# Another order, engine split and PSUM placement for a written-out schedule: two long convolutions and two MLPs on one core

## The chip, the cores and the metric

The kernel runs on one core of a Trainium2 chip. The core has five engines with a queue each: PE (TensorE, matrix products out of SBUF into PSUM), ACT (ScalarE), DVE (VectorE), POOL (GpSimd) and SP, which here only issues DMAs. PSUM has eight banks of 2 KB on each of 128 partitions. The metric is the time of one execution on the device in microseconds (us), lower is better. Three runs of the kernel before took 241.83, 242.24 and 243.01 us: the median is 242.24.

## What is computed

The reference, cut to the computation (S = 2048 tokens, D = 512 channels, FF = 1376, bf16 data):

```python
def _A_ref(q, k, v, shift_k, ssm_k, ssm_D):
    k_shift = sum over t in 0..3 of k_pad[:, t:t+S, :] * shift_k[:, 3 - t]
    kv = k_shift * v
    y = irfft(rfft(kv, 2S) * rfft(ssm_k, 2S))[:S]     # a causal convolution of length S
    y = y + kv * ssm_D
    return q * y

def _B_ref(x, w1, b1, w2, b2):
    y = _layernorm(x)
    h = gelu(y @ w1 + b1)
    return h @ w2 + b2

x = A_q
x = x + _A_ref(_layernorm(x), A_k, A_v, A_shift_k, A_ssm_k, A_ssm_D)
x = x + _B_ref(_layernorm(x), B_w1, B_b1, B_w2, B_b2)
x = x + _A_ref(_layernorm(x), A_k, A_v, A_shift_k, A_ssm_k, A_ssm_D)
x = x + _B_ref(_layernorm(x), B_w1, B_b1, B_w2, B_b2)
```

The convolution depends on k, v and the filter alone, so the kernel computes it once and uses it in both layers.

## The kernel before

**Recording and replay.** The program is not written engine by engine. The code calls `P.op(...)` 1114 times; each call records one operation (a group of matmuls, one evacuation, one vector operation, one DMA) with what it reads and writes, numbered in the order of the calls. `Prog.arrange` then goes through the tuple `ORDER`, a permutation of these numbers, and appends each operation to the queue of its engine. So `ORDER` alone sets the order within each of the five queues. Where an operation may run on either of two engines (`evac`, line 453, is given ACT and DVE), it takes the first, ACT, unless its number is in `SECOND`. `BANKS` gives each PSUM tile its first bank. `Prog.sync` works out the semaphore waits that this order needs, and `Prog.emit` writes the queues. Nothing is decided at run time.

**Stages, by their tags.**

- Loads: the filter ssm_k (four DMAs), k, v, the table S2 (`tab_s`, 16 DMAs), all issued by SP; a few small ones by ACT. Operation 4 (line 465) is `preload_act_table(Gelu_apprx_tanh)`; it reads and writes nothing that is tracked, so it has no predecessor and no successor.
- ht: four blocks of 16 transposes of the filter (line 528); taps: the shift filter spread over partitions (line 511).
- h1 (line 545, 16 groups of 16 small matmuls) and h2 (line 558, 16 groups of 8): the filter's transform in two steps. Each group fills two PSUM banks and is evacuated once by line 453, on ACT or DVE. Every group of h2 needs all groups of h1.
- Swap copies: 16 DMAs on SP (line 439, `ar<-ar`) copy the transformed filter with real and imaginary halves exchanged.
- fir0 to fir3: the short convolution of k and the product with v, for four groups of 128 channels. Channels 0 and 1 go over PE (transposes at line 589, evacuated by line 453; 14 matmuls at line 606 with taps that POOL prepares at line 520; a product at line 613 on DVE). Channels 2 and 3 are done on DVE (line 450), eight operations each.
- x1 (line 545) and x2 (line 651): the same transform for kv, in two halves of 64 channel groups. After each evacuation of x2, DVE multiplies by the filter and its swapped copy (line 450); the evacuations go through a ring of four buffers.
- i1 (line 674) and i2 (line 731): the inverse transform. Each half of i1 needs all products of its half.
- The MLP, in blocks of tokens, nine in layer 0 and four in layer 1: DVE normalizes (lines 754 to 768, with POOL at 760 and 762), the result is transposed (line 814 on PE for the first two token tiles, DMA transposes on SP at line 807 for the others), PE multiplies by w1 (line 827, 11 groups of 4, one PSUM bank each), ACT applies gelu with the bias (line 832), PE multiplies by w2 (line 860, 11 matmuls for a token tile), DVE adds the result to x (line 864). The last tile is done in three pieces (lines 849 and 853).

The lines that the change turns into another program:

Of the kernel before, what the change touches and what calls it, by code (L numbers as in the profile page):

```python
# [38 lines left out]
class Prog:  # L39
# [3 lines left out]

    G = 4
    ORDER = (
        49, 0, 47, 8, 7, 1, 3, 6, 48, 14, 71, 68, 5, 72, 18, 17, 15, 12, 4, 69, 9, 70, 50, 16, 65, 13, 19, 94, 2, 53, 73, 96, 51, 52, 11,
        92, 66, 305, 62, 95, 100, 97, 67, 104, 93, 63, 28, 64, 90, 88, 105, 10, 101, 26, 44, 45, 84, 91, 24, 56, 78, 85, 79, 86, 33, 59, 76,
        89, 57, 87, 198, 77, 36, 102, 168, 60, 103, 35, 25, 98, 30, 27, 31, 82, 74, 310, 182, 54, 169, 80, 61, 29, 183, 58, 199, 99, 37, 22,
        154, 75, 46, 81, 83, 172, 184, 42, 32, 155, 43, 120, 110, 116, 173, 121, 111, 34, 55, 112, 113, 39, 124, 158, 200, 125, 185, 20,
        106, 201, 108, 117, 23, 114, 107, 21, 38, 41, 159, 118, 109, 128, 156, 115, 136, 119, 122, 202, 40, 186, 203, 129, 157, 141, 204,  # L50
        132, 137, 133, 123, 134, 166, 170, 167, 187, 205, 130, 162, 171, 306, 144, 135, 126, 131, 127, 164, 138, 174, 163, 206, 175, 165,
        176, 207, 178, 139, 180, 140, 212, 179, 181, 160, 177, 188, 142, 213, 210, 295, 146, 208, 153, 209, 161, 189, 150, 211, 214, 148,
        223, 215, 224, 217, 147, 218, 151, 220, 192, 196, 193, 145, 194, 221, 149, 190, 197, 195, 235, 143, 225, 219, 226, 191, 236, 297,
        222, 304, 152, 229, 232, 230, 298, 296, 257, 216, 299, 227, 254, 237, 231, 233, 263, 228, 258, 264, 260, 234, 255, 269, 275, 259,
        252, 261, 303, 270, 253, 242, 294, 250, 243, 256, 265, 276, 262, 271, 246, 266, 272, 376, 277, 267, 300, 268, 248, 273, 274, 247,
        238, 249, 239, 333, 421, 240, 377, 334, 244, 251, 284, 241, 245, 477, 285, 311, 335, 288, 479, 289, 278, 313, 419, 336, 337, 314,
        338, 279, 378, 420, 286, 379, 287, 292, 380, 422, 290, 280, 339, 531, 293, 282, 342, 423, 478, 291, 529, 315, 281, 424, 283, 425,
        480, 302, 581, 316, 307, 381, 321, 323, 430, 331, 324, 325, 317, 322, 481, 329, 382, 340, 301, 326, 383, 341, 332, 308, 431, 482,
        343, 384, 426, 344, 385, 345, 386, 530, 346, 387, 347, 319, 388, 318, 432, 389, 330, 428, 348, 483, 349, 320, 390, 327, 354, 427,
        532, 391, 438, 328, 392, 368, 352, 533, 356, 309, 350, 355, 429, 364, 435, 433, 409, 360, 486, 357, 351, 358, 434, 353, 365, 436,  # L60
        439, 437, 362, 484, 363, 440, 485, 393, 487, 361, 394, 441, 397, 372, 410, 582, 395, 398, 366, 401, 489, 403, 442, 370, 359, 396,
        402, 534, 404, 367, 413, 407, 399, 443, 445, 538, 405, 411, 373, 583, 488, 635, 406, 400, 408, 312, 535, 491, 369, 490, 584, 371,
        492, 444, 414, 633, 415, 374, 416, 493, 446, 634, 494, 636, 497, 585, 586, 453, 536, 412, 454, 495, 590, 539, 451, 459, 637, 638,
        537, 465, 447, 591, 455, 466, 375, 461, 452, 540, 739, 449, 587, 642, 541, 592, 457, 498, 460, 450, 417, 448, 463, 496, 588, 643,
        543, 418, 462, 464, 507, 458, 509, 456, 542, 737, 685, 467, 589, 639, 503, 505, 499, 506, 544, 504, 515, 508, 469, 640, 468, 510,
        470, 593, 513, 687, 511, 473, 517, 545, 686, 738, 644, 740, 519, 546, 688, 689, 512, 549, 471, 550, 501, 690, 595, 516, 594, 596,
        547, 597, 502, 474, 514, 789, 548, 500, 641, 791, 598, 691, 694, 475, 525, 692, 521, 695, 551, 561, 518, 520, 567, 522, 476, 693,
        526, 599, 555, 645, 553, 696, 741, 742, 601, 552, 565, 527, 795, 554, 472, 646, 563, 566, 602, 743, 697, 562, 569, 557, 793, 746,
        571, 647, 699, 790, 600, 523, 568, 558, 570, 556, 524, 621, 648, 649, 572, 792, 744, 794, 559, 796, 698, 603, 560, 747, 611, 564,
        650, 651, 573, 609, 797, 607, 612, 700, 701, 748, 745, 605, 606, 652, 798, 653, 619, 528, 869, 608, 623, 620, 577, 615, 617, 802,  # L70
        702, 624, 799, 800, 613, 803, 574, 801, 749, 705, 654, 610, 706, 618, 614, 808, 751, 578, 703, 673, 669, 604, 575, 670, 576, 665,
        579, 622, 659, 667, 657, 750, 811, 616, 666, 809, 625, 871, 626, 661, 674, 675, 873, 870, 752, 872, 580, 753, 804, 660, 810, 662,
        754, 875, 874, 629, 876, 704, 805, 711, 658, 676, 806, 655, 725, 712, 663, 627, 812, 630, 817, 877, 878, 631, 709, 656, 668, 757,
        628, 888, 726, 671, 672, 758, 889, 813, 715, 681, 807, 716, 815, 885, 719, 755, 949, 723, 879, 664, 717, 724, 707, 632, 882, 682,
        886, 677, 756, 720, 816, 713, 883, 814, 880, 818, 881, 819, 683, 773, 951, 890, 678, 710, 820, 823, 684, 825, 827, 721, 950, 727,
        887, 759, 679, 884, 891, 892, 714, 761, 708, 824, 729, 821, 826, 718, 897, 762, 774, 769, 767, 680, 952, 728, 763, 895, 760, 896,
        953, 771, 779, 722, 730, 898, 775, 955, 822, 893, 770, 954, 765, 894, 956, 957, 733, 768, 958, 962, 828, 780, 777, 965, 899, 900,
        901, 731, 905, 734, 766, 968, 735, 764, 903, 839, 966, 963, 902, 785, 907, 831, 840, 776, 964, 732, 959, 906, 969, 781, 736, 960,
        778, 772, 845, 782, 973, 904, 908, 835, 843, 786, 787, 841, 1031, 967, 788, 929, 1029, 913, 846, 961, 970, 783, 784, 975, 1033,
        1035, 842, 844, 1030, 930, 836, 925, 976, 1032, 971, 911, 1034, 829, 849, 1036, 1037, 1038, 915, 912, 909, 972, 830, 923, 1045, 977,  # L80
        833, 832, 919, 974, 1046, 926, 978, 847, 979, 914, 1048, 834, 920, 1039, 980, 850, 1049, 1042, 1047, 985, 910, 916, 837, 917, 855,
        1040, 1041, 838, 851, 1043, 986, 1050, 987, 981, 864, 860, 918, 848, 927, 856, 1051, 921, 1044, 1052, 1055, 1056, 983, 1057, 984,
        1053, 940, 922, 924, 865, 852, 857, 982, 988, 853, 858, 944, 995, 1058, 928, 1054, 861, 991, 854, 1059, 862, 997, 1003, 1060, 945,
        992, 931, 946, 1061, 866, 941, 998, 1004, 1063, 1001, 1009, 1064, 932, 947, 942, 1062, 996, 1067, 1068, 943, 1065, 867, 935, 1005,
        1010, 1066, 1007, 936, 1002, 993, 1008, 1069, 999, 994, 989, 1000, 1085, 990, 933, 1081, 937, 1073, 1082, 1083, 1086, 948, 1020,
        1006, 1070, 1075, 1071, 938, 863, 1077, 1076, 1074, 1089, 1024, 934, 1087, 1072, 1100, 1084, 1078, 859, 1079, 1091, 1080, 1011,
        1095, 1090, 1101, 1088, 1015, 1111, 1012, 1016, 1021, 1102, 1017, 1092, 1025, 1103, 1112, 939, 1013, 1026, 1022, 1113, 1014, 1093,
        1027, 1096, 1097, 1094, 1104, 1105, 868, 1023, 1018, 1098, 1028, 1019, 1108, 1106, 1099, 1109, 1107, 1110)
    SECOND = (
        63, 64, 66, 67, 69, 72, 89, 97, 105, 127, 155, 161, 169, 175, 177, 215, 221, 239, 291, 349, 392)  # L90
    BANKS = (
        0, 4, 2, 2, 0, 2, 2, 0, 6, 6, 0, 0, 4, 2, 4, 4, 0, 6, 4, 0, 2, 6, 2, 0, 6, 0, 4, 4, 2, 0, 2, 2, 4, 6, 0, 6, 4, 4, 4, 0, 6, 0, 2, 0,
        0, 6, 6, 2, 6, 4, 0, 6, 4, 0, 2, 6, 2, 6, 4, 2, 0, 2, 4, 6, 6, 2, 4, 0, 6, 2, 4, 4, 2, 4, 0, 2, 2, 0, 4, 6, 4, 0, 6, 6, 6, 6, 0, 0,
        0, 2, 4, 2, 4, 2, 2, 0, 6, 0, 0, 2, 6, 4, 4, 1, 5, 4, 0, 4, 3, 0, 6, 2, 7, 0, 6, 6, 1, 1, 5, 3, 5, 3, 4, 5, 2, 2, 1, 3, 7, 2, 2, 1,
        5, 4, 0, 1, 2, 1, 2, 5, 1, 6, 2, 4, 5, 1, 7, 2, 7, 0, 4, 3, 7, 6, 2, 4, 1, 0, 1, 0, 4, 2, 3, 2, 5, 1, 7, 5, 7, 2, 4, 7, 6, 3, 2, 3,
        0, 6, 1, 0, 6, 4, 0, 5, 5, 5, 2, 2, 1, 6, 6, 0, 2, 6, 7, 5, 4, 4, 5, 4, 7, 1, 4, 2, 6, 5, 3, 4, 2, 4, 1, 4, 3, 1, 7, 0, 0, 6, 4, 5,
        1, 3, 5, 3, 2, 7, 0, 3, 0, 2, 3, 7, 1, 6, 7, 7, 4, 6, 2, 1, 2, 5, 0, 0, 2, 0, 5, 4, 5, 6, 0, 6, 7, 3, 2, 2, 2, 7, 4, 3, 5, 0, 3, 4,
        4, 7, 2, 4, 1, 1, 6, 6, 3, 0, 2, 6, 1, 7, 6, 0, 2)


    def __init__(self, nc):
# [799 lines left out]
```

## Time and profile before

| | |
|---|---|
| median of three runs | 242.24 us |
| the profiled execution, its own time | 240.63 us |
| span of its first to last instruction | 238.8 us |
| PE busy | 226.2 us, 95% |
| DVE busy | 171.6 us, 72% |
| ACT busy | 138.3 us, 58% |
| granted TensorE clock | 1.00 |
| PE's instruction queue (q8) | 18 packets, 0.29 MB |

A share of busy time is a mean over the stages. By the 40 slices of the page, DVE and ACT are full in the first third, and PE is full in the rest. In the views, "idle before" is the time in which an engine did nothing ahead of an instruction, with what ended it; "issue" means that the profile shows nothing that the engine waited for.

### The profile page before, as it was taken

What the parts mean: (1) busy time and instruction counts of PE and PEld (TensorE: products, weight loads), DVE (VectorE), ACT (ScalarE), POOL (GpSimd) and SP (SyncE); (2) the same over time, 40 slices, a digit from 0 to 9 for tenths busy, and PEclk for the clock granted to TensorE, in tenths of its full rate; (3) what the DMA queues carried; (4) which work ended last, traced back from release to release, by engine and by line L of the source; (5) the groups of instructions that cost most, each with busy time, mean ns of one, the idle gap of its engine ahead of it and who ended that gap; (6) DMA issues with size and microseconds to landing.
All of it is one profiled execution on the core that took longest, in us unless ns stands there. A gap on an engine that the chain in (4) does not pass through costs nothing.

```text
span 238.8 us, 5555 instructions
## 1 busy us (share of the span) xinstructions
PE 226.2 (95%) x2312; PEld 151.6 (63%) x2332; DVE 171.6 (72%) x359; ACT 138.3 (58%) x225; POOL 41.3 (17%) x77
## 2 busy tenths in 40 slices
PE   7987989886999999999999999999999999999995
PEld 3875778875899886766766667644444444444543
DVE  0979999999999999999887999693793312030035
ACT  2598799999999995642754444342782042454100
POOL 2179000000013444041230310400220200000000
PEclk9999999999999999999999999999999999999999
DMA  6999949999960003111122022240013021310024
GB/s 241 364 342 383 383 148 253 249 272 309 379 227 0 3 0 68 26 23 31 37 47 44 0 48 44 45 88 3 0 22 66 3 44 31 101 44 3 0 71 148
DMA packets 37035, 27.40 MB, mean 115 GB/s; under 512 B 19506, under 2 KB 29969, under 8 KB 37010
## 3 DMA queue, kind: packets, MB, share of 16 engines
q1 hardware_dynamic: 36446, 26.91, 37.8%
q8 instruction: 18, 0.29, 0.5%
q10 hardware_dynamic: 564, 0.14, 0.4%
q14 instruction: 7, 0.06, 0.1%
HBM read 16.82 MB, written 2.10 MB: 79 GB/s over the span
## 4 chain that ended last, share of the span: by engine, by line
PE 77%; ACT 9%; DMA 4%; DVE 4%; SPq 3%; issue 3%; ACTq 0%
PE ps L860 31%; PE ps L827 30%; ACT ar L453 9%; PE ps L674 5%; PE ps L731 3%; SPq L439 3%; PE ps L545 3%; DMA ar<-in_A_ssm_k_dram 2%; DVE ar L453 2%; DMA ar<-ar 2%; PE ps L528 1%; PE ps L606 1%; PE ps L849 1%; DVE sm L754 1%; PE ps L589 1%
## 5 line engine op out<-in xcount | busy, mean ns | idle before, releaser
L832 ACT ACTIVATE ar<-ps,sm 128x256 bf16<-128x256 f32 (+4 forms) x143 | 64.7, 525 | 72.5 <-PE ps L827 68.1
L827 PE MATMUL ps<-ar 128*128 128x256 bf16 (+4 forms) x568 | 84.2, 297 | 0.2
L860 PE MATMUL ps<-ar 128*128 128x512 bf16 (+1 forms) x329 | 79.0, 379 | 0.6
L453 ACT ACTIVATE ar<-ps 128x1024 bf16<-128x1024 f32 (+1 forms) x81 | 72.5, 1057 | 9.0 <-PE ps L511 4.5
L827 PEld LDWEIGHTS ps<-ar 128*128 128x128 bf16 (+1 forms) x572 | 52.9, 100 | 29.8 <-ACT ar L832 0.5
L450 DVE TENSOR_TENSOR ar<-ar 128x512 bf16<-128x512 bf16 (+3 forms) x106 | 63.6, 634 | 2.0 <-DMA ar<-in_A_k_dram 1.3
L860 PEld LDWEIGHTS ps<-ar 128*128 128x128 bf16 (+1 forms) x341 | 33.1, 98 | 34.3 <-ACT ar L832 0.3
L864 DVE TENSOR_TENSOR ar<-ar,ps 128x512 bf16<-128x512 bf16 x31 | 20.6, 680 | 47.3 <-PE ps L860 47.3
L754 DVE BATCH_NORM_STATS2 sm<-ar 128x6 f32<-128x512 bf16 (+1 forms) x68 | 42.8, 647 | 0.1
L768 DVE TENSOR_SCALAR ar<-ar,sm 128x512 bf16<-128x512 bf16 x64 | 25.0, 407 | 7.8 <-POOL sm L762 5.2
L760 POOL TENSOR_SCALAR sm<-sm 128x2 f32<-128x2 f32 (+2 forms) x26 | 6.0, 232 | 93.9 <-DVE sm L756 93.3
L762 POOL TENSOR_TENSOR sm<-sm 128x2 f32<-128x2 f32 (+2 forms) x26 | 21.6, 832 | 2.2
L545 PE MATMUL ps<-ar 128*64 128x128 bf16 x512 | 17.1, 221 | 1.4 <-issue 0.8
L545 PEld LDWEIGHTS ps<-ar 128*64 128x64 bf16 x512 | 14.9, 110 | 3.2 <-issue 1.0
L674 PE MATMUL ps<-ar 128*128 128x128 bf16 x256 | 15.0, 220 | 0.6 <-ACT ar L453 0.6
L674 PEld LDWEIGHTS ps<-ar 128*128 128x128 bf16 x256 | 14.7, 114 | 0.8 <-ACT ar L453 0.8
L453 DVE CAST ar<-ps 128x1024 bf16<-128x1024 f32 x11 | 13.0, 1212 | 0.3 <-PE ps L558 0.3
L651 PE MATMUL ps<-ar 128*128 128x64 bf16 x256 | 9.8, 194 | 3.2 <-ACT ar L453 2.7
L453 DVE COPY ar<-ps 128x2048 bf16<-128x2048 bf16 (+1 forms) x8 | 8.2, 1024 | 6.4 <-PE ps L528 6.3
L651 PEld LDWEIGHTS ps<-ar 128*128 128x128 bf16 x256 | 8.2, 98 | 4.7 <-ACT ar L453 3.9
L756 DVE BATCH_NORM_AGGREGATE sm<-sm 128x2 f32<-128x6 f32 (+1 forms) x64 | 9.9, 171 | 0.3
L558 PE MATMUL ps<-ar 128*128 128x128 bf16 x128 | 8.6, 220 | 0.8 <-ACT ar L453 0.8
(34 smaller groups left out, 78.1 us busy)
## 6 DMA issues: line engine op xcount, KB each, us to landing
ar<-tab_s SPq DMA_DIRECT2D x16, 256.0 KB, 9.6
ar<-ar SPq DMA_DIRECT2D x16, 256.0 KB, 4.2
ar<-in_A_ssm_k_dram SPq DMA_DIRECT2D x4, 512.0 KB, 5.3
ar<-in_A_k_dram SPq DMA_DIRECT2D x8, 256.0 KB, 7.6
ar<-in_A_v_dram SPq DMA_DIRECT2D x8, 256.0 KB, 9.6
ar<-in_A_q_dram SPq DMA_DIRECT2D x4, 512.0 KB, 7.9
out_dram<-ar SPq DMA_DIRECT2D x7, 256.0 KB, 2.1
ar<-in_B_w_dram SPq DMA_DIRECT2D x1, 1376.0 KB, 12.6
```

Of the source, the lines that this page charges most:

```text
L450: return P.op(eng, lambda e: e.tensor_tensor(o, a, b, op), reads=[a, b] + list(more), writes=[o])
L453: f = {ACT: lambda e: e.activation(dst, src(), AF.Copy), DVE: lambda e: e.tensor_copy(dst, src())}
L545: r = e.matmul(Q(tl, 64 * ri, 64, i * 128, [1, 128]), w, m, start=True, stop=True)
L651: r = e.matmul(Q(tl, 0, 128, i * pitch, [1, n]), w, m, start=True, stop=True)
L674: r = e.matmul(Q(tl, 0, 128, i * 128, [1, 128]), w, m, start=q == 0, stop=q == 1)
L754: P.op(DVE, lambda e, sj=sj, x=x: e.bn_stats(sj, x), reads=[x], writes=[sj])
L762: P.op(POOL, lambda e: e.tensor_tensor(r, v, hf, ALU.pow), reads=[v, hf], writes=[r])
L768: P.op(DVE, lambda e: e.tensor_scalar(o, x, m, r, ALU.subtract, ALU.mult), reads=[x, m, r], writes=[o])
L827: r = e.matmul(Q(tl, 0, rows, 0, [1, w]), a, m, start=dk == 0, stop=dk == 3)
L832: P.op(ACT, lambda e, dst=dst, tl=tl, rows=rows, bias=bias, w=w: e.activation(dst, Q(tl, 0, rows, 0, [1, w]), AF.Gelu_apprx_tanh, bias=bia ...
L860: r = e.matmul(Q(tl, 0, 128, 0, [1, 512]), ins[fc][0], ins[fc][1], start=fc == 0, stop=fc == 10)
L864: P.op(DVE, lambda e, x=x, tl=tl: e.tensor_tensor(x, x, Q(tl, 0, 128, 0, [1, 512]), ALU.add), reads=[x], writes=[x], tile=tl)
```

## The change

Three tuples of `Prog` are replaced: `ORDER`, `SECOND` and `BANKS`. No other line differs. The head of each, and the lines of `ORDER` in which operation 4 stands:

```diff
     ORDER = (
-        49, 0, 47, 8, 7, 1, 3, 6, 48, 14, 71, 68, 5, 72, 18, 17, 15, 12, 4, 69, 9, 70, 50, 16, 65, 13, 19, 94, 2, 53, 73, 96, 51, 52, 11,
-        92, 66, 305, 62, 95, 100, 97, 67, 104, 93, 63, 28, 64, 90, 88, 105, 10, 101, 26, 44, 45, 84, 91, 24, 56, 78, 85, 79, 86, 33, 59, 76,
...
+        47, 48, 7, 49, 0, 68, 1, 50, 69, 3, 6, 70, 8, 5, 65, 15, 18, 71, 2, 51, 66, 11, 52, 19, 90, 72, 67, 73, 53, 62, 91, 104, 17, 96, 63,
+        105, 14, 13, 98, 82, 12, 61, 16, 10, 64, 76, 34, 97, 21, 22, 77, 99, 28, 44, 83, 80, 84, 86, 59, 94, 85, 81, 78, 87, 79, 36, 23,
...
+        793, 504, 511, 740, 512, 690, 516, 563, 518, 571, 561, 513, 794, 694, 644, 507, 520, 647, 521, 562, 601, 599, 789, 602, 741, 691, 4,
...
     SECOND = (
-        63, 64, 66, 67, 69, 72, 89, 97, 105, 127, 155, 161, 169, 175, 177, 215, 221, 239, 291, 349, 392)
+        63, 64, 66, 67, 69, 72, 77, 85, 95, 97, 165, 169, 175, 181, 209, 218, 221, 279, 281, 349, 392)
     BANKS = (
-        0, 4, 2, 2, 0, 2, 2, 0, 6, 6, 0, 0, 4, 2, 4, 4, 0, 6, 4, 0, 2, 6, 2, 0, 6, 0, 4, 4, 2, 0, 2, 2, 4, 6, 0, 6, 4, 4, 4, 0, 6, 0, 2, 0,
+        0, 2, 4, 4, 0, 0, 4, 0, 2, 2, 4, 6, 4, 2, 2, 2, 0, 2, 6, 4, 6, 0, 2, 0, 4, 2, 0, 6, 0, 2, 2, 4, 6, 6, 4, 0, 0, 2, 6, 4, 2, 2, 6, 0,
```

What the numbers stand for: 47 to 49 memsets and the warm-up matmuls, 0 to 3 small loads of ACT, 5 to 8 the four loads of the filter, 10 to 27 k and v, 28 to 43 S2; 62, 65, 68 and 71 the blocks of ht; 74 to 104 (even) the matmuls of h1 and the odd number after each its evacuation; 106 to 136 (even) the same of h2. In `SECOND`, 77 to 105 are evacuations of h1, 127 one of h2, 155 that of the transposed keys of channel 0, 161 to 209 of x1 (169 of the keys of channel 1), 215 to 221 of x2, 239 to 291 of i1. Nine evacuations move from ACT to DVE and nine from DVE to ACT.

The first operations of PE's queue: before, the warm-up, ht 71, ht 68, taps 50, ht 65, h1 94, 96, 92, ht 62, h1 100. After: the warm-up, ht 68, taps 50, ht 65, ht 71, h1 90, ht 62, h1 104, 96, 98. The rest of the two queues holds the same stages in nearly the same succession; within h2, x1, x2, i1 and the MLP the groups are permuted, and groups of lines 827 and 860 are interleaved in other lengths.

In SP's queue the loads and the swap copies are permuted; the 30 DMA transposes follow as before, with neighbours exchanged. In ACT's queue, operation 4 no longer stands before the first evacuation but behind the gelu 562, in the fifth block of layer 0.

## Prediction

> **What bounds the kernel now.** I read the busy time by stretches first, to see where PE (TensorE) is idle at all.
>
> ```profile
> core 0: us, PE busy (x) PEld busy (x) DVE busy (x) ACT busy (x) POOL busy (x), PEclk, DMA share, GB/s
> 0.00:6.00 6.00, 4.44 (x24) 2.10 (x24) 0.00 (x0) 1.28 (x1) 1.64 (x7) 1.00 0.66 241
> 6.00:25.00 19.00, 16.48 (x357) 14.19 (x359) 16.92 (x17) 13.32 (x15) 10.60 (x14) 1.00 1.05 364
> 25.00:41.00 16.00, 14.80 (x227) 12.20 (x228) 15.65 (x14) 15.68 (x18) 0.00 (x0) 1.00 0.84 252
> 41.00:65.00 24.00, 19.92 (x523) 17.71 (x518) 24.00 (x23) 24.00 (x28) 0.52 (x1) 1.00 0.98 299
> 65.00:230.00 165.00, 164.16 (x1152) 101.74 (x1169) 110.45 (x300) 83.97 (x166) 28.56 (x55) 1.00 0.17 40
> ```
>
> Of 165 us after 65, PE is idle in 0.84 (165.00 - 164.16). Before 65 it is idle in 9.36 us (1.56 + 2.52 + 1.20 + 4.08), and there ACT and DVE are the full engines. So PE's remaining work, which the change keeps, follows 65 us without a hole: whatever moves that start moves the end, and a hole made later is not won back. The clock is 1.00 throughout.
>
> Next ACT's timeline, for how long ACT is without a gap.
>
> ```profile
> 16.21 6.52 ACT L453 ACTIVATE ar<-ps 128x1024 bf16<-128x1024 f32 x7 [0.22 <-PE ps L545]
> 25.32 45.05 ACT L453 ACTIVATE ar<-ps 128x1024 bf16<-128x1024 f32 x49 [2.58 <-PE ps L558]
> ...
> 78.17 6.58 ACT L453 ACTIVATE ar<-ps 128x512 bf16<-128x512 f32 x8 [0.21 <-PE ps L731]
> 84.56 4.22 ACT L832 ACTIVATE ar<-ps,sm 128x128 bf16<-128x128 f32 x15
> 89.24 1.89 ACT L832 ACTIVATE ar<-ps,sm 128x128 bf16<-128x128 f32 x7 [0.46 <-PE ps L827]
> ```
>
> From the first evacuation of h2 (25.32) to 88.78 ACT rests 0.21 us: 66 evacuations, then the first gelus (L832). The first gelu starts at 84.56, though its matmuls (L827) were done near 83.46: ACT is 1.1 us behind PE there.
>
> Then the chain of waits ahead of 25.32.
>
> ```profile
> 14.81 0.79 issue
> 15.60 1.47 PE ps L545 x45
> 17.07 1.00 PE ps L589 x16
> ...
> 20.77 1.31 issue
> 22.08 1.01 PE ps L589 x15
> 23.15 1.69 PE ps L606 x13
> 24.84 0.46 PE ps L558 x8
> ```
>
> The two "issue" pieces stand before PE's instructions 450 and 706 (a matmul counts as a weight load and a matmul). They are 256 instructions apart, and PE's instruction queue (q8: 18 packets, 0.29 MB) carries packets of 16,384 bytes, 64 bytes for each of 256 instructions. So a block begins at every 256k - 62. The packet records show when each is asked for: PE entered the block at 194 at 9.91, the packet for 450 ran 13.01 to 14.11, PE went on at 15.60; it entered 450 at 15.60, the packet for 706 ran 19.54 to 20.66, PE went on at 22.08. Each time: a wait of 3.10 and 3.94 for the packet, 1.1 in transfer, 1.4 to 1.5 until use. Later the wait for a packet was 4.48 (entry 22.08) and 0.09 (entry 31.89, loads done).
>
> [...]
>
> **The change part by part.** No operation is added or removed in the source: three tuples change, and with them order, engine and PSUM bank. The sum is made against the profiled execution (span 238.8, time 240.63); the median of the runs, 242.24, lies 1.61 above that, and I add the difference to the median.
>
> *The early order on PE.* Before: two blocks of ht (L528, 16 transposes each), taps (L511), ht, three of h1 (L545, 16 matmuls each), ht; instruction 194 is reached at 9.91. After: ht, taps, ht, ht, h1, ht, h1. Both blocks are 32 instructions, but one of ht takes 1.2 us (7.77 to 8.97) and one of h1 0.5. By the rows: ht 4.78 to 6.03, taps to 6.57, ht to 7.77, ht to 8.97, h1 to 9.5, ht to 10.7; instruction 194 at 10.8, which is 0.9 late. With the nearest waits (3.2, then 4.05 as the SP backlog grows) the next blocks come at 10.8 + 3.2 + 1.1 + 1.45 = 16.55 and 16.55 + 4.05 + 1.1 + 1.45 = 23.15, against 15.60 and 22.08. PE's own work between (128 matmuls at 33 ns, one L589 block) ends near 21.35, so the fetch still decides. After it stand the same L589 x16 and L606 x14 as before, and ACT's first h2 starts 3.24 later, at 26.4: **+1.07**. Bounds: with waits of 0.09 PE would not stall and h2 would start near 23.5 (-1.8); with 4.48 twice, 28.2 (+2.8). I take the rows nearest in time, since the same loads stand in SP's queue, in another order.
>
> *Evacuations that change engine* (18, nine each way). Transposed keys of channel 0 go from DVE to ACT: 2048 elements, by the slope of L832 (472 ns at 256, 686 at 512) 0.60 + 1536 x 0.836 ns = 1.9 us. They fall at 24.2 to 26.1, into ACT's wait for h2, at nothing; without that cover, +1.9. Between the first h2 and the first gelu ACT has 66 evacuations in either order. At 59.24 us for them (25.32 to 84.56), the shift of 1.07 carries on to the start of the full stretch and to the first gelu. DVE does 43 operations instead of 45 from the shift's first multiply to the last product, but begins 1.8 later (four h1 casts before it) and waits for the first product's evacuation, at 49.5 against 49.37: its last product ends near 68.9 against 68.21, and PE's L674 of the second half is due at 69.8. Nothing.
>
> *The swap copies on SP.* The half that needs the first eight columns of h2 starts after the thirteenth evacuation instead of the ninth (38.3 against 33.7), the other at 41.8. At 0.7 us each and 4.2 to landing, the first product's copies land at 48.9 (due 49.5), the last at 60.5 (due 64.1). Nothing, with 0.6 us of cover; the loads of x, w1 and w2 behind them land by 73 and are due after 68 (x) and 84.
>
> *The table load.* The operation that preloads the gelu table moves from the head of ACT's queue to a place after the first gelu of the fifth block. The changed program as built has three table loads instead of one: another set before the first copy, gelu's set before the first L832, gelu's set again at the moved place. The price is a row:
>
> ```profile
> L465 ACT ACT_TABLE_LOAD x1: 1283/1283/1283, 2.1 to 2.1; - x1
> ```
>
> The first falls into ACT's wait for taps (it was idle until 7.87): nothing. The second stands between the last i2 evacuation and the first gelu. There the queue behind it is all gelus, and PE waits for their banks: eight m1 tiles (one bank each) can be open, the ninth needs the first gelu's end. Shifted by 1.07, PE has eight open at 86.3; without the load the first gelu ends at 86.1, with it at 87.4 to 87.6. The five m1 tiles and the first m2 that follow each wait for the next gelu, so PE loses **+1.3** and has no idle time later to win it from. Bounds: 0 if ACT came there 1.3 earlier, 1.44 with the drain of one ACTIVATE (1.07 long, 0.91 apart). The third: PE has L860 x4, and two or three L827 groups (2.17 us) before it needs the gelu behind the load, which ends 1.9 to 2.0 after; hidden by 0.2, else up to +1.3.
>
> [...]
>
> *The MLP order, banks, POOL.* Norms that feed a block's first L827 have 3.2 to 5.9 us for their transposes by my count of DVE's and PE's work ahead of each (2.6 at the tightest before). POOL's eight L520 end by 21, the first user comes at 24.2. The last matmuls are the same three pieces. Nothing; if a norm were late by more than its cover, PE would wait by the excess.
>
> Sum: 1.07 + 1.3 = **+2.4**: span 241.2, median **244.6** (+1.0%).
>
> **The rivals.**
> 1. *The third load is bare too, or loads cost more than their row.* PE then waits again by about 1.3: 242.24 + 2.4 + 1.3 = 245.9. For it: cover of only 0.2. Against: L832 rests most of that time (ACT is busy in 24.24 of the 53 us from 107). [...]
> 2. *The fetches hide* (the other side, not slower). If a packet is served as at 31.89, 0.09 after the entry, the blocks come at 13.5 and 17.7, PE runs through, h2 starts 1.8 earlier and the load takes back 1.3: 241.7. It decides from waits under about 2 us. For it: one row; the order may meet thinner traffic. Against: every row from 10 to 27 us, at 369 GB/s. [...]
> 3. *The load at the first gelu is covered*, ACT being ahead of PE there: 242.24 + 1.07 = 243.3. Against: 66 evacuations in both, and ACT late by 1.1 already.
> 4. *The order does what it is named for:* fetches hide and the load is covered: 242.24 - 1.8 = 240.4. The blocks' places in the program cannot move, only the work around them; the walk above finds the same two stalls, the first longer.
>
> **How the numbers follow.** About 0.5% (1.2 us) can be told from no change. Chances: forecast 0.56 (its own range 243.4 to 245.6), rival 1 0.16, 2 0.11, 3 0.10, 4 0.07. Slower is the forecast and rival 1, less 0.02 at the edge: 0.70; same is 2, 3 and that edge, less a little for 2 below 241.0: 0.21; faster 0.09. The range takes in rivals 2 and 3 and most of 1: 241.4 to 246.8.
>
> **What would show it.** Three ACT_TABLE_LOAD rows, the second with L832 behind it; PE idle about 1.3 near 86 to 89, "<-ACT ar L832"; "issue" waits of about 1.5 and 1.8 near 15 and 21; the first h2 evacuation at 26.4; ACT without a gap from there. It is wrong if the second load finds ACT idle, if "issue" waits are gone, or if PE waits after 95 us for a norm.

## The result, and the profile after

The changed kernel took 245.60 us in the median of six runs (243.86 to 245.95); the kernel before took 241.96 in the six runs beside it. The ratio is 1.0138, 95% interval 1.0090 to 1.0186. Five more rounds later gave 245.82 against 242.12: 1.0150, interval 1.0091 to 1.0210. So the change costs 3.3 to 3.7 us. Two of the twelve runs of experiment b below (246.69 and 823.48 us) were slow ones and are left out of its median and its ratio. The profiled execution took 245.58 us, with a span of 243.8. The profiled execution of before (240.63) lies 1.3 under its median, so I take the worth of an edit from ratios to the runs of before beside it (0.001 is 0.24 us), and use the spans to find places.

The busy time by stretches of the changed kernel (columns as before):

```profile
0.00:6.00 6.00, 4.62 (x21) 2.10 (x22) 0.00 (x0) 1.28 (x1) 0.92 (x6) 1.00 0.62 232
6.00:25.00 19.00, 16.01 (x355) 13.69 (x353) 16.77 (x16) 13.54 (x15) 8.78 (x14) 1.00 1.04 359
25.00:41.00 16.00, 15.23 (x208) 12.02 (x206) 15.06 (x15) 15.54 (x18) 0.34 (x2) 1.00 0.60 191
41.00:65.00 24.00, 18.60 (x506) 16.48 (x507) 22.30 (x20) 23.24 (x26) 0.00 (x0) 1.00 0.97 279
65.00:230.00 165.00, 162.86 (x1179) 101.17 (x1177) 113.49 (x302) 88.50 (x171) 28.36 (x55) 1.00 0.20 48
```

Before, DVE and ACT were full (24.00 each) in the stretch from 41 to 65. Here DVE rests 1.70 and ACT 0.76 in it, and PE is idle for 5.40 instead of 4.08. After 65 PE is idle for 2.14 instead of 0.84. So two places lost time: one in 41 to 65, one behind it. The first was not in the forecast. (The profile of before holds 2312 of PE's 2332 matmuls, that of the changed kernel all of them, so before's idle time may be a little less than these figures.)

The groups of ACT's table loads, by line (count, then busy time, then mean ns, then idle time before them), and ACT's timeline around h2 and around the first gelu:

```profile
L453 ACT ACT_TABLE_LOAD x1 | 1.3, 1283 | 2.5 <-issue 2.5
L832 ACT ACT_TABLE_LOAD x1 | 1.3, 1283 | 0.0
L465 ACT ACT_TABLE_LOAD x1 | 1.3, 1283 | 0.0
```

```profile
23.86 1.88 ACT L453 ACTIVATE ar<-ps 128x2048 bf16<-128x2048 bf16 x1 [0.74 <-PE ps L589]
26.05 3.77 ACT L453 ACTIVATE ar<-ps 128x1024 bf16<-128x1024 f32 x4 [0.31 <-PE ps L558]
...
83.31 3.81 ACT L453 ACTIVATE ar<-ps 128x1024 bf16<-128x1024 f32 x4
87.14 1.28 ACT L832 ACT_TABLE_LOAD   x1
88.43 3.20 ACT L832 ACTIVATE ar<-ps,sm 128x128 bf16<-128x128 f32 x12
```

There are three loads of 1283 ns. The second stands bare between the last evacuation of i2 and the first gelu: ACT has no gap on either side of it. The evacuation that came over from DVE (23.86) takes 1.88 us inside ACT's wait for h2, and h2 begins at 26.05.

PE's timeline at the places where it waits:

```profile
11.06 4.28 PE L545 MATMUL ps<-ar 128*64 128x128 bf16 x130
16.45 1.92 PE L545 MATMUL ps<-ar 128*64 128x128 bf16 x62 [1.10 <-issue]
...
22.76 1.07 PE L589 MATMUL ps<-ar 128*128 128x128 bf16 x16 [1.51 <-ACT ar L453]
...
55.80 1.57 PE L651 MATMUL ps<-ar 128*128 128x64 bf16 x48 [0.97 <-ACT ar L453]
57.64 0.64 PE L651 MATMUL ps<-ar 128*128 128x64 bf16 x16 [0.26 <-ACT ar L453]
59.03 0.64 PE L651 MATMUL ps<-ar 128*128 128x64 bf16 x16 [0.76 <-ACT ar L453]
61.37 1.95 PE L674 MATMUL ps<-ar 128*128 128x128 bf16 x32 [1.70 <-ACT ar L453]
...
85.65 2.15 PE L827 MATMUL ps<-ar 128*128 128x128 bf16 x32
88.85 1.43 PE L827 MATMUL ps<-ar 128*128 128x128 bf16 x20 [1.06 <-ACT ar L832]
...
134.64 1.48 PE L827 MATMUL ps<-ar 128*128 128x256 bf16 x12 [0.53 <-DVE ar L864]
...
144.62 1.04 PE L860 MATMUL ps<-ar 128*128 128x512 bf16 x4 [0.26 <-DVE ar L864]
```

Both stalls for a block of instructions are still there (16.45 and 22.76; the second carries ACT's name, but its packet landed at 21.44, 1.3 before use; at the first, and at both of the kernel before, that lag was 1.4 to 1.5). PE opens eight m1 tiles (x32) and then waits 1.06 for the first gelu's end. Two waits for line 864 are new. The waits at 59.03 and 61.37 come from DVE. Here are PE at line 674 and DVE in the kernel before, then DVE and a piece of the chain of waits in the changed kernel:

```profile
59.42 3.83 PE L674 MATMUL ps<-ar 128*128 128x128 bf16 x64 [0.28 <-ACT ar L453]
49.37 14.84 DVE L450 TENSOR_TENSOR ar<-ar 128x2048 bf16<-128x2048 bf16 x13
```

```profile
52.89 2.35 DVE L450 TENSOR_TENSOR ar<-ar 128x2048 bf16<-128x2048 bf16 x2
56.64 10.31 DVE L450 TENSOR_TENSOR ar<-ar 128x2048 bf16<-128x2048 bf16 x9 [1.39 <-DMA ar<-ar]
```

```profile
47.64 2.79 SPq L439
...
51.15 5.46 DMA ar<-ar
56.61 0.02 issue
```

DVE's product (operation 231) waits 1.39 us for its swap copy (operation 147), which SP issued at 51.15 and which landed at 56.6. The ring of x2 buffers then holds up ACT (0.4 us), and ACT holds up PE (0.76 and 1.70).

### The profile page after: what moved, and what is told of

It reads as the page before. It is cut to its first block, busy times and chain, and to the rows that moved or that the text cites. A ratio compares the mean times of both kernels' runs of the same rounds, so it can differ in the third digit from the quotient of the medians.

```text
span 243.8 us, 5581 instructions
## 1 busy us (share of the span) xinstructions
PE 228.6 (94%) x2332; PEld 151.6 (62%) x2332; DVE 172.4 (71%) x359; ACT 142.4 (58%) x227; POOL 38.4 (16%) x77
## 4 chain that ended last, share of the span: by engine, by line
PE 61%; DVE 12%; SPq 11%; DMA 8%; ACT 5%; issue 2%; POOL 1%; DVEq 0%; POOLq 0%; ACTq 0%
PE ps L827 28%; PE ps L860 27%; DVE ar L450 7%; SPq L439 6%; PE ps L674 5%; SPq L447 4%; ACT ar L453 4%; DMA ar<-ar 4%; DMA ar<-in_A_v_dram 4%; DVE sm L754 1%; DVE ar L768 1%; PE ps L849 1%; DVE ar L453 1%; DVE ar L613 1%; PE ps L731 1%
## 5 line engine op out<-in xcount | busy, mean ns | idle before, releaser
L832 ACT ACTIVATE ar<-ps,sm 128x256 bf16<-128x256 f32 (+5 forms) x143 | 64.5, 525 | 76.1 <-PE ps L827 70.9
L827 PE MATMUL ps<-ar 128*128 128x256 bf16 (+5 forms) x572 | 84.4, 298 | 1.6 <-ACT ar L832 1.1
L860 PE MATMUL ps<-ar 128*128 128x512 bf16 (+1 forms) x341 | 81.1, 380 | 0.3 <-DVE ar L864 0.3
L453 ACT ACTIVATE ar<-ps 128x1024 bf16<-128x1024 f32 (+2 forms) x81 | 74.0, 1047 | 9.3 <-PE ps L545 3.8
L762 POOL TENSOR_TENSOR sm<-sm 128x2 f32<-128x2 f32 (+2 forms) x26 | 21.1, 811 | 2.2
L545 PE MATMUL ps<-ar 128*64 128x128 bf16 x512 | 17.7, 221 | 2.4 <-ACT ar L453 1.3
L453 DVE CAST ar<-ps 128x1024 bf16<-128x1024 f32 x12 | 14.5, 1221 | 1.5 <-PE ps L545 1.2
L453 DVE COPY ar<-ps 128x2048 bf16<-128x2048 bf16 (+1 forms) x7 | 7.0, 999 | 6.9 <-PE ps L528 6.6
```

What stands on the lines that cost most here:

```text
L453: f = {ACT: lambda e: e.activation(dst, src(), AF.Copy), DVE: lambda e: e.tensor_copy(dst, src())}
L545: r = e.matmul(Q(tl, 64 * ri, 64, i * 128, [1, 128]), w, m, start=True, stop=True)
L762: P.op(POOL, lambda e: e.tensor_tensor(r, v, hf, ALU.pow), reads=[v, hf], writes=[r])
L827: r = e.matmul(Q(tl, 0, rows, 0, [1, w]), a, m, start=dk == 0, stop=dk == 3)
L832: P.op(ACT, lambda e, dst=dst, tl=tl, rows=rows, bias=bias, w=w: e.activation(dst, Q(tl, 0, rows, 0, [1, w]), AF.Gelu_apprx_tanh, bias=bia ...
L860: r = e.matmul(Q(tl, 0, 128, 0, [1, 512]), ins[fc][0], ins[fc][1], start=fc == 0, stop=fc == 10)
```

## The experiments

All ratios are to the kernel before, run beside the experiment on the same chip. Operation numbers are those of the recording.

**a: the changed kernel, with the table load back at the head.**

```diff
-        ... 3, 6, 70, 8, ...              ... 741, 691, 4, ...
+        ... 3, 4, 6, 70, 8, ...           ... 741, 691, ...
```

> The changed kernel with one edit: operation 4 (the preload of gelu's table) is put back to the head of ACT's queue, so that one table load is left. Theory: the load at the first gelu costs what PE waits there, 1.06 us in the profile of the changed kernel, and the third load is hidden: the time falls by 1.0 to 1.3 us to about 244.4, the span by as much, and PE's wait for the first gelu goes. Rival: ACT is late at the first gelu for other reasons, the wait stays at over half and the time falls by less than 0.5 us. Rival: both loads cost in full, then it falls by 2.5 us.

244.79 us, 1.0101 (1.0050 to 1.0152). PE no longer waits for the first gelus; the first gelu follows the last evacuation at once. Against the changed kernel (1.0138 and 1.0150) the gain is 0.9 to 1.2 us, within wide intervals. DVE's wait for the swap copy stays (1.23), and with it what c shows.

**b: the kernel before, with the load behind gelu 562.**

```diff
-        ... 12, 4, 69, 9, ...
+        ... 743, 697, 562, 4, 569, ...
```

> The kernel before with one edit: operation 4 stands behind the gelu 562, as in the changed kernel; the built program then has three table loads. Theory: ACT is 1.1 us behind PE at the first gelu, so a load of 1.28 there makes PE wait about 1.1 to 1.3 us: 242.0 becomes 243.2. Rival: it is covered, and the time stays within 0.4 us. [...]

243.6 us in the median of ten runs, 1.0082 (1.0051 to 1.0113). ACT's and PE's timelines of b:

```profile
85.50 1.28 ACT L832 ACT_TABLE_LOAD   x1
86.80 4.08 ACT L832 ACTIVATE ar<-ps,sm 128x128 bf16<-128x128 f32 x15
```

```profile
84.31 1.85 PE L827 MATMUL ps<-ar 128*128 128x128 bf16 x28
87.22 1.17 PE L827 MATMUL ps<-ar 128*128 128x128 bf16 x16 [1.06 <-ACT ar L832]
```

The order of PE is that of before, so the starts can be compared operation by operation. Up to here b is 0.4 to 0.7 late. At this wait the delay jumps from 0.72 to 1.96, with the groups behind it to 2.10, and it stays. At the third load it grows by another 0.49. By its ratio the load alone costs 2.0 us, a little more than these two steps (1.87 together) and more than the 1.1 to 1.3 that were expected. The interval of that ratio is 1.2 to 2.7 us. ACT starts the first gelu 0.02 after the load's end.

**c: the changed kernel, with the 16 swap copies in the order in which the products need them.** Their places in SP's queue are the same; only which copy stands in which place differs.

```diff
-        142, 138, 139, 149, 141, 140, 146, 143, 151, 144, 148, 147, 145, 152, 150, 153
+        138, 139, 140, 141, 146, 147, 148, 149, 142, 143, 144, 145, 150, 151, 152, 153
```

> The changed kernel with one edit: the sixteen swap copies keep their sixteen places in SP's queue, but stand in the order in which the products need them (138 to 141, 146 to 149, then 142 to 145, 150 to 153). Theory: DVE's wait of 1.39 us for the copies of the second quarter, at 56.6, goes, the ring of four buffers no longer holds ACT, and the full stretch of PE starts 0.8 to 1.4 us earlier: time about 244.5. Rival: DVE's wait is hidden behind ACT, which is full there, and the time stays within 0.4 us.

243.63 us, 1.0086 (1.0059 to 1.0113), against 1.0138 and 1.0150 of the changed kernel: a gain of 1.3 to 1.5 us, more than expected. DVE and PE of c:

```profile
52.29 14.84 DVE L450 TENSOR_TENSOR ar<-ar 128x2048 bf16<-128x2048 bf16 x13
```

```profile
57.95 0.64 PE L651 MATMUL ps<-ar 128*128 128x64 bf16 x16 [0.28 <-ACT ar L453]
59.28 1.95 PE L674 MATMUL ps<-ar 128*128 128x128 bf16 x32 [0.69 <-ACT ar L453]
...
86.95 1.43 PE L827 MATMUL ps<-ar 128*128 128x128 bf16 x20 [1.06 <-ACT ar L832]
```

DVE now does 13 products in a row without a gap, as in the kernel before, and PE's wait before line 674 falls from 1.70 to 0.69. The wait for the gelus is untouched. TensorE's clock differs too. In each of c's 12 runs the mean granted clock was 1.0; in the changed kernel it was 0.993 in 9 of 12, in a, on c's chip, 0.992 or 0.993 in 4 of 6. Here is the changed kernel's second profile, by windows and on PE's timeline:

```profile
60.00:62.00 2.00, 1.94 (x19) 1.97 (x20) 2.00 (x2) 1.89 (x2) 0.00 (x0) 0.50 1.06 353
62.00:64.00 2.00, 2.00 (x37) 2.00 (x35) 2.00 (x3) 0.56 (x2) 0.00 (x0) 0.66 1.04 407
```

```profile
57.94 0.64 PE L651 MATMUL ps<-ar 128*128 128x64 bf16 x16 [0.28 <-ACT ar L453]
60.06 3.50 PE L674 MATMUL ps<-ar 128*128 128x128 bf16 x32 [1.48 <-ACT ar L453]
```

At the end of PE's wait the granted clock falls to 0.50, and 32 matmuls take 3.50 us instead of 1.95. So the late copy costs its own wait and, in 9 of 12 executions by their mean clock, a stretch at half clock, which adds 1.55 us here. Of the changed kernel's first six runs, the two shortest (243.86 and 243.99) had the full clock, the profiled one (245.58) too, and the other three 0.993.

**d: a and c together.**

> The changed kernel with both edits (operation 4 at the head, swap copies in the order of need). Theory: they add up, 2.0 to 2.6 us less than the changed kernel: about 243.2, which leaves the late front (h2 starts at 26.05 instead of 25.32) and the waits of PE for L864. Rival: they overlap, since ACT is the late engine in both, and the second gives less than half of its own.

242.06 us, 1.0022 (0.9993 to 1.0051). Both repairs bring the time back to that of before, as far as the interval tells, and together give more than was expected: 2.8 to 3.1 us by the ratios. Against c, on the same chip, the load's return is worth 1.57 us of median. Between the two profiles PE's order is the same, so the starts can be compared. c's delay against d rises at the first gelus from 0.32 to 1.54, and to 1.73 with the groups behind (1.41 in all); the third load adds 0.05. Near 131 us the delay falls by 0.48, because d waits 0.56 for line 864 there and c does not. So this pair keeps 0.98 of the load's 1.46.

Against a, on the same chip too, only the order of the swap copies differs, and it is worth 1.9 us by the ratios. a's two runs at full clock (243.00 and 243.10) lie 1.0 above d's median, its four at 0.992 or 0.993 (244.60 to 245.06) 2.5 to 3.0 above. So in a the wait costs about 1.0, and the half clock about 1.9 where it comes.

```profile
83.80 1.10 ACT L453 ACTIVATE ar<-ps 128x1024 bf16<-128x1024 f32 x1
84.71 3.30 ACT L832 ACTIVATE ar<-ps,sm 128x128 bf16<-128x128 f32 x12
```

This is ACT in d: no load, and the gelus 1.8 us earlier than in c.

**e: d with the first 109 operations of before** (with their engines and banks, and eight later tiles in other banks for that), meant to isolate the early order.

> The kernel of d_both with the first 109 operations of the order (loads, ht, h1, the first matmuls of fir) in the sequence and on the engines of the kernel before; eight later tiles get another PSUM bank so that the two parts fit. The prediction said that the front of the changed kernel costs 1.07 us: then this is 1.0 us faster than d_both, 241.0. Rival, by the profiles so far (h2 starts at 25.1 to 26.1 with the new front, at 25.3 and 25.7 with the old one): the front costs nothing and the time is that of d_both, 242.1 within 0.4.

251.96 us, 1.0401: no answer to its question. Before's load order does not serve the later order of h2 and fir; two of PE's waits:

```profile
29.80 1.07 PE L558 MATMUL ps<-ar 128*128 128x128 bf16 x16 [1.84 <-DMA ar<-tab_s]
33.14 1.04 PE L558 MATMUL ps<-ar 128*128 128x128 bf16 x8 [2.28 <-DVE ar L613]
```

It suggests only that SP's load order and PE's order behind it belong together.

**i: d up to the first m1, then the order and banks of before.** **j: the reverse, before up to the first m1, then the changed order.** Both ask what the MLP's order is worth.

> The kernel of d_both up to the first m1 matmul, and from there the order and banks of the kernel before. Theory: what d_both still loses to the kernel before (0.6 us) are PE's waits of 0.56 and 0.26 us for L864 near 131 and 141 us, so it goes: 241.3, no such waits. Rival: it lies ahead of the first m1; then the time stays at 242.1.

> The kernel before up to the first m1 matmul, and from there the order and banks of the changed kernel, with the table load at the head. Theory: PE waits 0.5 to 0.8 us for L864, and the time is 0.6 us above the kernel before, 242.1. Rival: nothing, 241.5.

i took 242.33 us, 1.0024 (0.9997 to 1.0050), j 243.81, 1.0082 (1.0054 to 1.0111). PE of i and then of j where the two orders meet:

```profile
84.70 3.10 PE L827 MATMUL ps<-ar 128*128 128x128 bf16 x48 [0.44 <-ACT ar L453]
```

```profile
85.16 3.08 PE L827 MATMUL ps<-ar 128*128 128x128 bf16 x52 [1.06 <-ACT ar L453]
```

In i the waits for line 864 are gone, but a wait of 0.44 at the join takes their place, and the time is that of d. In j a wait of 1.06 at the join is half of the loss of 2.0, and waits of 0.31 and 0.25 for line 864 are left. The MLP's first banks fit the i2 order ahead of them, so neither splice prices the MLP's order cleanly.

**k: the kernel before, with the changed kernel's order of swap copies.**

> The kernel before with one edit: the sixteen swap copies stand in the order of the changed kernel, in the places that they have before. Theory: the fourth of them waits for the last evacuation of h2, the copies for the second quarter of the products come after four others, DVE waits 1 us or more for them, PE idles over 1 us in the stretch from 50 to 62, and the half clock for one stretch of 3.4 us comes in more of the runs than 2 of 29: 242.5 to 244. Rival: in the kernel before the copies start 4.7 us earlier, which covers it: 241.5.

241.78 us, 1.0004 (0.9976 to 1.0032). DVE of k:

```profile
54.74 10.31 DVE L450 TENSOR_TENSOR ar<-ar 128x2048 bf16<-128x2048 bf16 x9 [0.55 <-DMA ar<-ar]
```

The same order of copies costs only 0.55 on DVE, and nothing that the time shows (the interval is 0.7 us wide to either side). The first copy leaves at 33.9 in k and at 38.4 in the changed kernel, but that head start does not reach copy 147: the fourth copy of this order (149) needs the last evacuation of h2, which ends at 41.64 in k and at 42.00 in the changed kernel, and every later copy stands behind it in SP's queue. What differs is the way from there. From the issue of 149 to the landing of 147 it takes 13.0 us in k, 13.9, 14.4 and 14.6 in the changed kernel's second profile, in a and in the changed kernel's first profile; their waits on DVE are 0.55, 0.69, 1.23 and 1.39. Most of that spread is one issue, that of copy 144, two places ahead of 147: 1.12, 1.72, 2.69 and 2.79 us. Why it takes so long stays open. So the order alone makes a wait; its size varies from execution to execution, and the first start does not set it.

**l: the kernel before, with the last block of ht ahead of three groups of h1.** **m: the same, with other banks for that block.**

```diff
-        ... 65, 13, 19, 94, ... 92, 66, 305, 62, 95, ...
+        ... 65, 13, 19, 66, 62, 94, ... 92, 305, 95, ...
```

> The program before with one edit: the last block of the filter's transposes (op 62, line 528) and the evacuation that frees its bank (66) stand ahead of the first three groups of h1, so PE reaches instruction 194 later by 0.7 (a block of ht takes 1.2 us, one of h1 0.5), as in the changed kernel. Forecast's theory: the packet's wait (3.1) starts at the entry, so the blocks come 0.7 later at 16.3 and 22.8, the first evacuation of h2 at 26.0 instead of 25.3, the time +0.7 to +0.9 (ratio 1.003). Rival: the packet starts near 13.0 to 13.6 whatever the entry, because it stands behind the loads already in the rings; then the wait shrinks to about 2.6, the first evacuation of h2 stays within 0.3 and the time within 0.3 (ratio 0.999 to 1.001).

> The same edit as in l_front on the program before, with other PSUM banks (op 62's tile in banks 6 and 7, those of 78, 88, 96 and 104 exchanged for it), so that op 62 no longer waits 1.32 us for a bank: instruction 194 is reached near 10.8 instead of 9.9. If the packet's wait starts at the entry, as l_front's 2.88 after an entry of 12.2 says, the blocks come near 16.3 and 22.8, the first evacuation of h2 near 26.0 to 26.2, and the time is +0.7 to +0.9 (ratio 1.003 to 1.004). If a small delay of the entry is absorbed (packet near 13.2 whatever the entry up to some 11), the first evacuation of h2 is within 0.3 of 25.3 to 25.7 and the time within 0.3.

l took 244.67 us, 1.0099 (1.0064 to 1.0134), m 243.25, 1.0066 (1.0032 to 1.0100). PE of l and of m:

```profile
10.56 1.23 PE L528 MATMUL ps<-ar 128*128 128x128 bf16 x16 [1.32 <-DVE ar L453]
...
17.71 1.48 PE L545 MATMUL ps<-ar 128*64 128x128 bf16 x46 [0.63 <-issue]
```

```profile
10.07 1.23 PE L528 MATMUL ps<-ar 128*128 128x128 bf16 x16 [1.07 <-DMA ar<-in_A_ssm_k_dram]
...
17.00 1.51 PE L545 MATMUL ps<-ar 128*64 128x128 bf16 x45 [0.36 <-issue]
```

Neither gave the delay of 0.7 that was meant. In l the block waits for a bank, in m for its load, and the entry into the block of instruction 194 comes at 12.25 and 11.76. But they do tell how such a delay goes on. From the packet records (us):

| execution | entry | wait for the packet | next block used | the one after | first h2 evacuation |
|---|---|---|---|---|---|
| front of before, 4 profiles (before, b, j, k), mean | 10.12 | 3.12 | 15.78 | 22.22 | 25.54 |
| changed front, 6 profiles (the kernel twice, a, c, d, i), mean | 10.88 | 2.69 | 15.94 | 22.25 | 25.55 |
| of these, the changed kernel's first profile | 11.09 | 2.83 | 16.45 | 22.75 | 26.05 |
| l | 12.25 | 2.88 | 17.71 | 23.93 | 27.94 |
| m | 11.76 | 2.82 | 17.00 | 23.31 | 29.01 |

Entries that come 2.13 and 1.64 later than the mean of before's front move the next block by 1.93 and 1.22. So the packet does not stand ready at a fixed time, and a late entry does cost. (m's h2 is later than l's because another stretch at half clock fell there (0.50 from 26 to 28 us): its line 606 took 2.90 us for 13 matmuls instead of 1.69.)

## Why the prediction came out as it did

The forecast was 244.6, the measurement 245.60: slower as forecast, by 3.3 to 3.7 us (1.4% to 1.5%) instead of 2.4 (1.0%). One term of the sum was right, one was too large, and a step put at nothing was not nothing. The last two errors partly cancel, so that the number came this near is in part luck. The time also lies near that of rival 1 (245.9), whose mechanism, a bare third load, did not happen in the changed kernel.

- **The second table load, +1.3: right.** ACT came to the first gelus without slack, PE had eight tiles open, waited 1.06, and its delay grew by 1.41 (d to c) and 1.38 (before to b) over the groups that wait for a gelu; the upper bound in the prediction was 1.44. The edit is worth 1.57 (medians of d and c) and 2.0 (ratio of b), the third load included. In the changed kernel's trace nothing stands beside the load's own 1.28: the evacuation before it ends at 87.12, the load runs from 87.14 to 88.42, the gelu starts at 88.43.
- **The third load, "hidden by 0.2": right for the changed order.** It showed 0.05 there (d to c). In b, with the MLP order of before, it showed 0.49. Rival 1 put 1.3 on it.
- **The early order on PE, +1.07: the mechanism stands, the term was too large.** The entry came 0.76 later by the means (0.9 forecast). The failed step is "With the nearest waits (3.2, then 4.05 as the SP backlog grows)": the packet's wait was 2.69 in the mean, 0.43 shorter than with the old front, not 0.1 longer. With slightly shorter lags behind it, the second block was used at 22.25 against 22.22, and h2 began at 25.55 against 25.54. In the profiled pair the shift was 0.73; over all profiles it is nothing. l and m show that a larger delay would have gone through. Rival 2, fetches that hide, did not come: both stalls stayed.
- **The swap copies, "Nothing, with 0.6 us of cover": wrong.** Two things in that step failed. It compared the first and the last copy with their due times, and the late one was the twelfth in SP's row, needed by the fifth product, which DVE could have begun at 55.24. And its rates, 0.7 us for an issue and 4.2 to landing, were too low for this copy. The issues on SP's queue of before, and then of the changed kernel (minimum, median and maximum in ns; first and last start):

```profile
L439 SPq DMA_DIRECT2D ar<-ar x16: 600/658/1452, 33.7 to 51.1; - x16
```

```profile
L439 SPq DMA_DIRECT2D ar<-ar x16: 595/664/2785, 38.4 to 58.1; - x16
```

  The median is as I had it, but single issues take up to 2.8 us. The fourth copy, 149, was issued at 42.02, when the last evacuation of h2 was done (41.8 in the prediction); eight issues and a load of x (0.64) then stand ahead of copy 147. At 0.7 and 4.2 it would have landed near 52.5 (42.02 + 8 x 0.7 + 0.64 + 4.2), 2.8 us before its use. The eight issues took 8.11 us, 1.01 each, so that it left at 51.15; it took 5.46 to land, at 56.61, and DVE waited 1.39. The changed kernel against c prices the step at 1.3 to 1.5 us by ratios, a against d at 1.9, the half clock included.
- **Engine swaps, at nothing: right where it was priced.** The keys' evacuation took 1.88 us (1.9 forecast) in ACT's wait for h2. The other seventeen, and the new banks, were not run alone; they are part of what d keeps.
- **The MLP's order, "Nothing": not settled.** No norm was late, as argued, but PE waits 0.53 and 0.26 for line 864, which the step did not look at. i removed these waits and gained nothing that the interval shows, with 0.44 lost at the join.

The 3.3 to 3.7 us are then: 1.3 to 1.5 for the swap copies (the changed kernel to c), 1.6 for the load (c to d), and 0.5 (d to before), whose interval, -0.2 to 1.2, includes nothing. In the other order the load is worth 0.9 to 1.2 (the changed kernel to a) and the swap copies 1.9 (a to d); each of these steps has an interval of about 1 us to either side. The last piece, 0.5, holds all else that changed and stays open; the waits for line 864 are a candidate that i did not confirm. No version that was run is faster than the kernel before.

## What to carry to other kernels

When a row of transfers feeds a row of consumers, compare each landing with its own use, not the first and the last, and walk the queue with the mean of its issues, stragglers included, and with the landing times of that stretch. An early first transfer did not help those that stood behind one which still had to wait: in k the first copy left 4.5 us sooner than in the changed kernel, but copy 149, with the later ones behind it, waited for an evacuation that ended at 41.64 instead of 42.00. A preload that depends on nothing still has a best place: here, moved behind the first use of what it loads, it left three loads of 1283 ns instead of one, and the second stood where the consumer has no slack (PE waited 1.06 us). A delay seen in one profiled pair (0.7 us at h2 here) should be set against several profiles before it is put into a sum.

## What the runs showed that was not expected

In the changed kernel's second profile a wait of 1.48 us on PE was followed by about as much again in lost clock: PE was busy for 0.58 of the 2 us before 60, behind that the granted clock is 0.50, and 32 matmuls took 1.55 us longer; in this trace and in those of a and m the half clock lasted for 3.41 or 3.42 us, in that of e for 6.83, twice as long. In the first profile PE was busy for 1.55 of the 4 us before 62, and the clock stayed at 1.00. The mean clock was 0.992 or 0.993 in 13 of 18 runs of the two kernels with a DVE wait of 0.69 or more for a swap copy (the changed kernel and a), in none of 36 runs of c, d and i, in 3 of 12 of k (wait of 0.55), and in 17 of 92 runs of before, whose profile shows none. b, j, l and m, without such a wait, had it in 10 of 48, and all six runs of e, with other waits on PE, lay at 0.993 or below. The counts of before differ from chip to chip too: beside a, c and d before had it in 2 of 29 runs, beside i and k in 6 of 29, beside the later six of the changed kernel in 5 of 17. All of those six had it, where about half were expected, and three of the first six. Runs at 0.993 of the changed kernel have a median of 245.84; two of its three others lie at 243.9. The longest gap ahead of the half clock was 1.48 us in the second profile and 1.69 in that of a, with PE working a little ahead of it. The first profile has a gap of 1.70 there and kept the full clock, so the gap's length alone does not decide it. Why the half clock comes in some executions only stays open.
